# A fused top-k attention and two-layer MLP kernel: the norm's product and low part on GpSimd, another order of VectorE's group, the third transpose in a score bank, layer 2's inputs later

## The chip, the cores and the metric

One Trainium2 chip, one of its cores. A time is the device time of one execution in microseconds (us). The engines are PE (TensorE), DVE (VectorE), ACT (ScalarE), POOL (GpSimd) and SP (SyncE, which here only issues transfers).

## The reference, cut to what matters

```python
def _attn_ref(q, k, v):                       # q, k, v: 4 x 8 x 576 x 64, fp32
    scores = (1 / sqrt(64)) * q @ k.T
    kth = 32nd largest score of each row
    scores = where(scores >= kth, scores, -1e9)
    attn = exp(scores - max(scores))
    attn = attn / (sum(attn) + 1e-9)
    return attn @ v                           # then 2304 tokens x 512
def _moe_ref(x, w_in, w_out, a, b):           # 512 -> 2048 -> 512
    h = x @ w_in
    P = a[0] + a[1]*h + a[2]*h**2 + a[3]*h**3
    Q = 1 + abs(b[0])*abs(h) + abs(b[1])*h**2
    return (P / (Q + 1e-6)) @ w_out
def _moe2_ref(x, w_in, w_out):                # 512 -> 2048 -> 512
    h = x @ w_in
    return (h * cos(h)) @ w_out
```

## The kernel before, in words

Attention runs as 72 **units**: a unit is 128 query rows (tile `t` of two) of a pair of heads (`pr` of four) in one of nine blocks `k` of 256 tokens, so eight units make a block. `qk(i)` forms a unit's scores in `sx`, two PSUM banks that stay in use for the whole kernel: the left half of the 576 keys in bank 0, the right half in bank 1, 288 columns each, first for one head, then for the other; ACT copies them to `sS`. `topk(i)` works on DVE: it writes the elementwise max and min of the two halves into `e`, then alternates MAX8 and MATCH_REPLACE8 four times (the "rank" instructions) until the 32nd value stands, ACT writes exp into `e`, and two SCALAR_TENSOR_TENSOR instructions, the "masks", keep what reaches the 32nd value and sum it. `av(i)` transposes `e` on PE (four 128x128 pieces `pp..a`, four `pp..b` and one, the third, `pp..t`), ACT copies each result to SBUF (`pt..`), and the products with `v` go to free columns of `sx` and from there, through ACT, to `xst` (tile `xs`). After every fourth unit `norm` divides by the row sums: `rs` (DVE), spread to `rx` (ACT), transposed to `bc` on PE in PSUM, `xs` times `bc` (DVE), then a rounded part `xh` (ACT) and the rest `xl`.

The two layers run in groups of 256 hidden columns, one group `g` of each layer per unit, each layer some units behind the attention that feeds it. `mm_in` (lines 480 to 491) is 24 matmuls: `in1` for layer 1, `in2` for layer 2. Layer 1's rational function is `in1`, `pol1`, `mid1` and `end1` (four SCALAR_TENSOR_TENSOR on DVE that end in `u`, "the cubic"; ACT then rounds `u` to `gg`), `low1`, and `out1`, 24 matmuls into `y`. Layer 2's is `in2`, `mid2` (on DVE, behind three ACT steps that end in `n`), a sine on ACT for two groups at a time, `mul2`, `low2`, and `out2`, 12 matmuls into `o`.

**What sets the order.** Every unit has five pieces, p 0 to 4. A table (`timed`, lines 657 to 671) gives each step of the two layers a piece; the attention is a generator that yields once per piece, and a scheduler keeps each engine's order near the order in which code is written. Units 20 to 71 (`U0`, `U1`) are **grouped**: in each, DVE runs its "shared" instructions (max, min, cubic, masks, `mid2`) in one run in the order of the code, then the rank instructions, and every POOL instruction waits for the last shared instruction written before it (classes `InOrder` and `Behind`).

**What waits in queues.** The weights that aren't kept in SBUF come through a ring of four 512 KB buffers (`stream`, tag `st`), filled by SP in the order in which the steps stand in the table: one load each for `in1` (`lo0`), `in2` (`lo1`) and `out1` (`w1ol`), two for `out2` (`w2o`). A load waits until the load four before it has been used. `ps_t` is a ring of two PSUM banks (tag `h`) that `in1`, `in2`, `pp..a`, `pp..b`, `pp..t` and `bc` take in turn; each waits until what stood there two before has been copied out.

Of the kernel before, what the change touches and what calls it, by code (L numbers as in the profile page):

```python
# [10 lines left out]
F32 = mybir.dt.float32  # L11
# [3 lines left out]
AF = mybir.ActivationFunctionType  # L15
# [8 lines left out]
P = 128  # L24
# [4 lines left out]
HALF = S // 2  # L29
# [5 lines left out]
BT = 2 * P  # L35
# [95 lines left out]
def body(tc, out, qt, kt, vt, ident_d, w1_d, w1o_d, a_d, b_d, w2_d, w2o_d):  # L131
# [5 lines left out]
    with ExitStack() as ctx:  # L137
# [186 lines left out]
        def after(mm, bank):  # L324
            for x in order[bank]:
                tc.add_manual_dep(mm.ins, x, mybir.DependencyInfo(mybir.DependencyClass.NoSync, mybir.DependencyReason.DATA), reason="bank")
# [76 lines left out]
        def av(i):  # L403
            n, pr = units[i]
            kvs = ins.pop(i)
            m = P // len(kvs)
            e = et.pop(i).rearrange("p a c -> p (a c)")
            kb, t, bank = n // 2, n % 2, i % 2
            if i % 4 == 0:
                xst[kb, pr // 2] = mo.tile([P, 2, BT], F32, tag="xs", bufs=XB, name=f"xs{kb}_{pr}")  # L410
            xp = sx[:, bank, HALF:HALF + P]

            def tr4(base, nm):
                pp = ps_t.tile([P, 4, P], F32, tag="h", name=f"pp{i}{nm}")
                for c in range(4):
                    PE.transpose(pp[:, c, :], e[:, base + c * P:base + (c + 1) * P], ident)
                pt = att.tile([P, 4, P], F32, tag="pts", bufs=2, name=f"pt{i}{nm}")
                A.activation(pt, pp, AF.Copy)
                return pt

            pj = [tr4(0, "a"), tr4(640, "b")]
            pp = ps_t.tile([P, P], F32, tag="h", name=f"pp{i}t")
            PE.transpose(pp, e[:, 512:640], ident)
            pt = att.tile([P, P], F32, tag="ptt", bufs=1, name=f"pt{i}t")
            A.activation(pt, pp, AF.Copy)
            last = []
            for c, (_, v) in enumerate(kvs):
                qs = slice(c * m, (c + 1) * m)
                mm = PE.matmul(xp[:, qs], v[:, 512:640], pt[:, qs], start=True, stop=False, skip_group_check=True)
                after(mm, bank)  # L430
                for kc in range(4):
                    for j in range(2):
                        o = xp[j * D:(j + 1) * D, qs]
                        mm = PE.matmul(o, v[:, kc * P + j * D:kc * P + (j + 1) * D], pj[j][:, kc, qs], start=False, stop=(kc == 3), skip_group_check=True)  # L434
                        after(mm, bank)
                        if kc == 3:
                            last.append(mm.ins.name)
            order[bank] = last
            A.activation(xst[kb, pr // 2][:, pr % 2, t * P:(t + 1) * P], xp, AF.Copy)

        def norm(kb, hf):
            rs = sml.tile([P, 2, H // 2], F32, tag="rs", bufs=2, name=f"rs{kb}_{hf}")
            V.tensor_scalar_add(rs, sums[kb][:, :, 4 * hf:4 * hf + 4], 1e-9)
            V.reciprocal(rs, rs)
            rx = sml.tile([P, 2, 2, P], F32, tag="rx", bufs=1, name=f"rx{kb}_{hf}")
            A.activation(rx.rearrange("p t c (j d) -> p (t c j) d", j=2), rs.rearrange("p t h -> p (t h)").unsqueeze(2).to_broadcast([P, 8, D]), AF.Copy)
            yield
            bc = ps_t.tile([P, 2, BT], F32, tag="h", name=f"bc{kb}_{hf}")
            for t in range(2):
                for c in range(2):  # L450
                    PE.transpose(bc[:, c, t * P:(t + 1) * P], rx[:, t, c], ident)
            yield
            x = xst.pop((kb, hf))
            V.tensor_mul(x, x, bc)
            yield
            if hf == 0:
                xhl[kb] = [mo.tile([P, NCC, BT], F32R, tag=t, name=f"{t}{kb}") for t in ("xh", "xl")]
            hi, lo = (t[:, 2 * hf:2 * hf + 2] for t in xhl[kb])
            A.activation(hi, x, AF.Copy)
            yield  # L460
            V.tensor_sub(lo, x, hi.bitcast(F32))

        lot, w1t, w2t = {}, {}, {}

# [193 lines left out]
        for k in range(NB):  # L658
            for g in range(NG):
                s1 = S0 + 40 * k + 5 * g  # L660
                s2 = s1 + 5 * LB
                if grouped1(k, g):
                    timed += [(s1, in1, k, g), (s1 + 5, pol1, k, g), (s1 + 9, end1, k, g), (s1 + 10, low1, k, g), (s1 + 11, out1, k, g)]
                else:
                    timed += [(s1, in1, k, g), (s1 + MD, mid1, k, g), (s1 + 5 * L1 - E1P, end1, k, g), (s1 + 5 * L1 + O1P, out1, k, g)]
                if grouped2(k, g):
                    timed += [(s2, in2, k, g), (s2 + 4, mid2, k, g), (s2 + 10, mul2, k, g), (s2 + 12, low2, k, g), (s2 + 13, out2, k, g)]
                else:
                    timed += [(s2 + I2, in2, k, g), (s2 + 5 * L2 + O2, out2, k, g), (s2 + M2P[g % SINB], mul2, k, g)]
            timed.append((s1 + 5 * L1 + SB, sub1, k, 0))  # L670
# [46 lines left out]
        def attention():  # L717
            load_k(1)
            load_v(0)
            qk(0)  # L720
            prev = None
            nrm, fresh, held, low, sq = [], [], [], [], None
            for i in range(nu + 1):
                if LQ == 0 and i % 2 == 0 and i + 2 < nu:
                    load_q(i + 2)
                if i + 1 < nu:
                    qk(i + 1)
                if i + 2 < nu:
                    load_k(i + 2)
                for x, a in held:  # L730
                    store_k(x, *a)
                held = [(prep(*a), a) for a in preps.get(i, [])]
                t = topk(i) if i < nu else iter([None] * 9)
                grouped = U0 <= i < U1
                for p in range(5):
                    if p == 0 and prev is not None and not grouped:
                        next(prev)
                    next(t, None)
                    if p == 0:
                        if grouped:  # L740
                            yield
                            next(prev)
                        if prev is not None:
                            next(prev)
                        if not grouped:
                            next(t, None)
                        for x in low:
                            next(x, None)
                        low = []
                        if prev is not None:  # L750
                            av(i - 1)
                            if i % 4 == 0:
                                nrm.append(norm((i - 1) // 8, (i - 1) // 4 % 2))
                                next(nrm[-1])
                                fresh.append(nrm[-1])
                                if not grouped:
                                    next(nrm[-1])
                        if 0 < i < nu:
                            load_v(i)
                    if p == LQ > 0 and i % 2 == 0 and i + 2 < nu:  # L760
                        load_q(i + 2)
                    if p == SQ and i % 2 == 0 and 8 <= i + 2 < nu:
                        sq = split_q(i + 2)
                        next(sq, None)
                    if p == SQ + 1 and sq is not None:
                        next(sq, None)
                        sq = None
                    if fresh and p == 1 and not grouped:
                        next(fresh.pop())
                    if fresh and grouped and p >= 3:  # L770
                        next(fresh[0])
                        if p == 4:
                            fresh.pop()
                    if len(nrm) == 2 and (p == 1 or p == 4):
                        if not grouped:
                            x = nrm[0 if p == 1 else 1]
                            next(x)
                            next(x, None)
                            if p == 4:
                                nrm = []  # L780
                        elif p == 4:
                            for x in nrm:
                                next(x)
                            low, nrm = nrm, []
                    yield
                prev = t

# [60 lines left out]
```

## Time and profile before

| | |
|---|---|
| median of 3 runs | 1506.75 us (1504.02 to 1507.62) |
| the profiled execution | 1508.62 us, span 1506.8 us |
| PE busy, mean granted clock | 1264.4 us (84%), 0.917 |
| DVE / ACT / POOL busy | 1177.0 / 1092.1 / 549.0 us (78 / 72 / 36%) |
| chain that ended last, by engine | PE 56%, DMA 19%, DVE 15%, ACT 6% |

Matmuls are pipelined, so a busy PE isn't PE at its peak, and PE's clock has two levels, 1.2 and 2.4 GHz: a granted clock of 0.5 is the lower one for the whole stretch. The elementwise work of DVE, ACT and POOL carries line 81, a helper's; its instructions are told apart by their tiles.

### The profile page before, as it was taken

The numbers are of one execution on the slowest core, as the hardware profiler recorded it, in microseconds if no ns is written. First come the engines' busy times: TensorE is split into PE (matmuls) and PEld (weight loads), VectorE is DVE, ScalarE is ACT, GpSimd is POOL, SyncE is SP. The second block draws the span as 40 slices with busy tenths as digits, with TensorE's granted clock in tenths as the row PEclk, the third lists the DMA queues.
The fourth block names the chain that finished last, engine by engine and source line by source line (L and its number), as shares of the span: only waits on it lengthen the run. The fifth ranks groups of instructions, "written<-read, shape, count | busy, mean of one in ns | idle before, by whom it ended". The sixth has DMA issues, their size and how long they took to land.

```text
span 1506.8 us, 24893 instructions
## 1 busy us (share of the span) xinstructions
PE 1264.4 (84%) x8944; PEld 1125.3 (75%) x8944; DVE 1177.0 (78%) x2503; ACT 1092.1 (72%) x1873; POOL 549.0 (36%) x413
## 2 busy tenths in 40 slices
PE   5765776558888988888879888888989898999998
PEld 2443555558777888888878878887878887899986
DVE  6999878998959795979596959786978796947633
ACT  6876877757676777777767778686867776868743
POOL 3566544532434333334333334342433333431000
PEclk9766987778998999999999999999999999999999
DMA  7887768854466655455655564554555776656787
GB/s 245 301 275 228 226 218 269 277 171 139 140 205 200 203 174 200 162 197 173 236 185 194 167 219 168 183 179 172 185 174 199 234 247 232 207 200 226 251 268 234
DMA packets 141548, 314.98 MB, mean 209 GB/s; under 512 B 12016, under 2 KB 28528, under 8 KB 141424
## 3 DMA queue, kind: packets, MB, share of 16 engines
q1 hardware_dynamic: 122832, 261.99, 52.4%
q10 hardware_dynamic: 18592, 51.39, 10.5%
q8 instruction: 71, 1.16, 0.3%
q14 instruction: 53, 0.43, 0.1%
HBM read 278.20 MB, written 35.13 MB: 208 GB/s over the span
## 4 chain that ended last, share of the span: by engine, by line
PE 56%; DMA 19%; DVE 15%; ACT 6%; issue 3%; POOL 1%; ACTq 0%; SPq 0%; DVEq 0%; POOLq 0%
DMA w1ol<-w1ol 11%; PE h L488 9%; PE o L628 9%; PE h L490 8%; PE h L489 8%; DVE e L81 7%; PE y L560 5%; PE y L558 4%; PE sx L434 4%; PE y L559 4%; DVE hd L81 3%; DVE cb L81 2%; DMA raw<-w 2%; DMA out<-ob 2%; DVE u L81 2%
## 5 line engine op out<-in xcount | busy, mean ns | idle before, releaser
L81 DVE MAX8 hd<-e 128x8 f32<-128x288 f32 (+1 forms) x576 | 321.1, 596 | 0.0
L81 DVE MATCH_REPLACE8 e<-hd,e 128x288 f32<-128x288 f32 (+1 forms) x432 | 231.0, 541 | 0.0
L558 PE MATMUL y<-gg,w1o 128*128 128x256 f32 x576 | 177.6, 308 | 54.4 <-ACT gg L81 54.4
L81 POOL TENSOR_TENSOR gg<-u,gg 128x512 fp32r<-128x512 f32 x64 | 83.9, 1311 | 380.3 <-DVE rr L81 93.9
L628 PE MATMUL o<-w2o,gg 128*128 128x512 f32 x864 | 219.4, 394 | 1.6 <-DMA w2o<-w2o 1.5
L560 PE MATMUL y<-gg,w1ol 128*128 128x256 f32 x576 | 175.4, 305 | 51.3 <-DMA w1ol<-w1ol 51.3
L559 PE MATMUL y<-gg,w1o 128*128 128x256 f32 x576 | 174.1, 302 | 6.7 <-POOL gg L81 6.7
L628 PEld LDWEIGHTS o<-w2o,gg 128*128 128x128 f32 x864 | 155.0, 189 | 30.4 <-DMA w2o<-w2o 2.2
L81 DVE TENSOR_TENSOR e<-sS 128x576 f32<-128x576 f32 x144 | 122.7, 891 | 63.8 <-ACT sS L81 58.7
L488 PE MATMUL h<-x2h,w2hi 128*128 128x256 f32 x576 | 167.6, 291 | 2.7 <-ACT pt28b L81 1.3
L488 PE MATMUL h<-xh,w1hi 128*128 128x256 f32 x576 | 169.8, 295 | 0.0
L490 PE MATMUL h<-x2h,lo 128*128 128x256 f32 x576 | 165.1, 287 | 0.3 <-DMA lo<-w2lo 0.3
L490 PE MATMUL h<-xh,lo 128*128 128x256 f32 x576 | 164.9, 286 | 0.0
L489 PE MATMUL h<-xl,w1hi 128*128 128x256 f32 x576 | 164.8, 286 | 0.0
L489 PE MATMUL h<-x2l,w2hi 128*128 128x256 f32 x576 | 164.8, 286 | 0.0
L558 PEld LDWEIGHTS y<-gg,w1o 128*128 128x128 f32 x576 | 118.8, 206 | 59.3 <-ACT gg L81 58.6
L560 PEld LDWEIGHTS y<-gg,w1ol 128*128 128x128 f32 x576 | 118.1, 205 | 59.3 <-DMA w1ol<-w1ol 58.5
L81 POOL TENSOR_TENSOR rr<-rr,hs 128x512 f32<-128x512 f32 x56 | 72.7, 1300 | 166.8 <-DVE rr L81 145.6
L81 POOL TENSOR_TENSOR cb<-cb,raw 128x512 int32<-128x512 int32 x64 | 93.0, 1454 | 99.1 <-DVE cb L81 69.5
L81 DVE SCALAR_TENSOR_TENSOR e<-sS,hd,e 128x576 f32<-128x576 f32 x144 | 125.2, 898 | 4.3 <-ACT e L81 4.2
L559 PEld LDWEIGHTS y<-gg,w1o 128*128 128x128 f32 x576 | 118.0, 205 | 9.5 <-POOL gg L81 9.2
L81 ACT ACTIVATE sS<-sx 128x576 f32<-128x576 f32 x144 | 93.1, 647 | 34.4 <-PE sx L348 15.9
(1167 smaller groups left out, 3641.5 us busy)
## 6 DMA issues: line engine op xcount, KB each, us to landing
w2o<-w2o SPq DMA_DIRECT2D x144, 512.0 KB, 4.4
lo<-w1lo SPq DMA_DIRECT2D x72, 512.0 KB, 4.4
w1ol<-w1ol SPq DMA_DIRECT2D x72, 512.0 KB, 4.6
lo<-w2lo SPq DMA_DIRECT2D x72, 512.0 KB, 4.0
k<-kdr ACTq DMA_DIRECT2D x44, 576.0 KB, 4.8
raw<-w SPq DMA_DIRECT2D x32, 512.0 KB, 5.2
v<-vt ACTq DMA_DIRECT2D x48, 320.0 KB, 4.3
qr<-qt ACTq DMA_DIRECT2D x36, 256.0 KB, 4.2
```

What stands on the lines that cost most here:

```text
L81: r = f(*a, **k)
L434: mm = PE.matmul(o, v[:, kc * P + j * D:kc * P + (j + 1) * D], pj[j][:, kc, qs], start=False, stop=(kc == 3), skip_group_check=True)
L488: PE.matmul(h[:, i, :], wh, xh[:, c, :], start=(c == 0), stop=False)
L489: PE.matmul(h[:, i, :], wh, xl[:, c, :], start=False, stop=False)
L490: PE.matmul(h[:, i, :], lo[:, i, c, :], xh[:, c, :], start=False, stop=(c == NCC - 1))
L558: PE.matmul(y[:, c, :], w1o[:, f, cs], gh[:, i, :], start=(f == 0 and c % 2 == 0), stop=False, skip_group_check=True)
L559: PE.matmul(y[:, c, :], w1o[:, f, cs], gl[:, i, :], start=False, stop=False, skip_group_check=True)
L560: PE.matmul(y[:, c, :], wl[:, i, cs], gh[:, i, :], start=False, stop=(f == NF - 1), skip_group_check=True)
L628: PE.matmul(o[:, t, :], l[:, i, ts], wt[i][:, r], start=(f == 0 and r == 0 and l is gh), stop=(f == NF - 1 and l is gl), skip_group_check= ...
```

## The change

Four edits. **Norm**: in the grouped units ACT copies `bc` from PSUM to an SBUF tile `bs`, and the product and the low part move from DVE to POOL; `bc` is written in p 0 instead of p 3, the product stays in p 4, and the low part comes in p 4 instead of the next unit's p 0. **Group order**: cubic, masks, max, min instead of max, min, cubic, masks. **Third transpose**: it goes to free columns of the score bank that the unit's output does not use, not to the `ps_t` ring. **Layer 2's inputs**: `in2` of grouped units stands two pieces later, so its load falls behind that of `out1`.

```diff
-            pp = ps_t.tile([P, P], F32, tag="h", name=f"pp{i}t")
-            PE.transpose(pp, e[:, 512:640], ident)
+            pp = sx[:, 1 - bank, HALF:HALF + P]
+            mm = PE.transpose(pp, e[:, 512:640], ident)
+            after(mm, 1 - bank)
+            order[1 - bank] = [mm.ins.name]
...
+            pool_norm = U0 <= 8 * kb + 4 * hf + 4 < U1
+            if pool_norm:
+                bs = sml.tile([P, 2, BT], F32, tag="rx", bufs=1, name=f"bs{kb}_{hf}")
+                A.activation(bs, bc, AF.Copy)
             yield
             x = xst.pop((kb, hf))
-            V.tensor_mul(x, x, bc)
+            if pool_norm:
+                G.tensor_mul(x, x, bs)
+            else:
+                V.tensor_mul(x, x, bc)
...
             A.activation(hi, x, AF.Copy)
-            yield
-            V.tensor_sub(lo, x, hi.bitcast(F32))
+            (G if pool_norm else V).tensor_sub(lo, x, hi.bitcast(F32))
...
-                    timed += [(s2, in2, k, g), (s2 + 4, mid2, k, g), (s2 + 10, mul2, k, g), (s2 + 12, low2, k, g), (s2 + 13, out2, k, g)]
+                    timed += [(s2 + I2, in2, k, g), (s2 + 4, mid2, k, g), (s2 + 10, mul2, k, g), (s2 + 12, low2, k, g), (s2 + 13, out2, k, g)]
...
-                    if p == 0 and prev is not None and not grouped:
+                    if p == 0 and grouped:
+                        yield
                         next(prev)
-                    next(t, None)
-                    if p == 0:
-                        if grouped:
-                            yield
-                            next(prev)
+                        next(prev)
+                        next(t)
...
-                    if fresh and grouped and p >= 3:
-                        next(fresh[0])
+                    if len(nrm) == 2 and (p == 4 or p == 1 and not grouped):
+                        for x in nrm if grouped else nrm[:1] if p == 1 else nrm[1:]:
+                            next(x, None)
```

In DVE's order where unit 44 ends and unit 45 begins, `ql46` is the split of a later unit's queries, `xs5_0` the norm's product, `e45` with `sS45` max and min, `u4_2` and `q4_2` the cubic, `e44,sum5` the masks. Before:

```order
L81 TENSOR_TENSOR ql46_8076<-qr46_7964,qh46_8075 128x512
L81 TENSOR_TENSOR xs5_0_7326<-xs5_0_7326,bc5_0_8078 128x512
L81 TENSOR_TENSOR e45_8122<-sS45_7896 128x2x288 x2
L81 SCALAR_TENSOR_TENSOR u4_2_7838<-u4_2_7838,nega_105,w4_2_7835 128x512
L81 SCALAR_TENSOR_TENSOR q4_2_7836<-q4_2_7836,r4_2_7837 128x512
L81 SCALAR_TENSOR_TENSOR u4_2_7838<-u4_2_7838,nega_105,r4_2_7837 128x512
L81 SCALAR_TENSOR_TENSOR u4_2_7838<-q4_2_7836,u4_2_7838 128x512
L81 SCALAR_TENSOR_TENSOR e44_7909,sum5_7092<-sS44_7702,hd_44_7910,e44_7909 128x576 x2
L81 SCALAR_TENSOR_TENSOR rr3_0_7797<-n3_1_8000,rr3_0_7797 128x512
```

and now, at the same place of DVE's queue:

```order
L81 TENSOR_TENSOR ql46_8019<-qr46_7939,qh46_8018 128x512
L81 SCALAR_TENSOR_TENSOR u4_2_7774<-u4_2_7774,nega_105,w4_2_7771 128x512
L81 SCALAR_TENSOR_TENSOR q4_2_7772<-q4_2_7772,r4_2_7773 128x512
L81 SCALAR_TENSOR_TENSOR u4_2_7774<-u4_2_7774,nega_105,r4_2_7773 128x512
L81 SCALAR_TENSOR_TENSOR u4_2_7774<-q4_2_7772,u4_2_7774 128x512
L81 SCALAR_TENSOR_TENSOR e44_7886,sum5_7071<-sS44_7672,hd_44_7887,e44_7886 128x576 x2
L81 TENSOR_TENSOR e45_8100<-sS45_7865 128x2x288 x2
L81 SCALAR_TENSOR_TENSOR rr3_0_7840<-n3_1_8051,rr3_0_7840 128x512
```

The norm's product is gone from the queue, and the cubic follows the rank instructions directly.

In ACT's order around unit 43's transposes and the norm (`rx5_0`, `bs5_0`), the change has these rows, where before `rx5_0` stood a few rows ahead of the copies and there was no `bs`:

```order
L81 ACTIVATE xs5_0_7298<-sx_91 128x128
L81 ACTIVATE rx5_0_7921<-rs5_0_7918 128x512
L81 ACTIVATE pt43a_7896<-pp43a_7891 128x512
L81 ACTIVATE pt43b_7903<-pp43b_7898 128x512
L81 ACTIVATE sS45_7865<-sx_91 128x576
L81 ACTIVATE nb_44_7888<-hd_44_7887 128x2
L81 ACTIVATE bs5_0_7928<-bc5_0_7923 128x512
```

On PE `bc5_0` now stands right behind unit 43's transposes and half of a score product, ahead of `in1`; before it stood inside `out2`, behind `out1`, `in2` and `in1`. So PE needs `rx` early, and the copy that `rx` holds up on ACT is the one that empties the ring for `bc` and `in1`.

On SP, the loads of one unit before (PE uses them in the order `w1ol`, `lo1`, `lo0`, `w2o`, `w2o`):

```order
L467 DMA lo1_3_1_7808<-w2lo_116 128x2x512
L467 DMA lo0_4_3_7847<-w1lo_115 128x2x512
L467 DMA w1ol4_1_7882<-w1ol_118 128x2x512
L467 DMA w2o2_14_7969<-w2o_119 128x1024
L467 DMA w2o2_15_7971<-w2o_119 128x1024
```

and now (PE uses them in the order `lo0`, `w1ol`, `lo1`, `w2o`, `w2o`):

```order
L475 DMA lo0_4_3_7783<-w1lo_115 128x2x512
L475 DMA w1ol4_1_7813<-w1ol_118 128x2x512
L475 DMA lo1_3_1_7851<-w2lo_116 128x2x512
L475 DMA w2o2_14_7949<-w2o_119 128x1024
L475 DMA w2o2_15_7951<-w2o_119 128x1024
```

`lo1` has moved from first to third. `w1ol`, which before took the buffer of the last unit's first `w2o`, now takes that of the last unit's `lo1`.

## Rows read from the trace of the kernel before

**Rows 1.** Busy us (x instructions) of each engine by stretch, PE clock, DMA share, GB/s.

```profile
378.00:1320.00 942.00, 826.86 (x6284) 767.91 (x6283) 752.71 (x1677) 693.36 (x1176) 348.31 (x266) 0.95 0.58 193
1320.00:1507.00 187.00, 178.40 (x1255) 164.69 (x1253) 94.27 (x141) 115.78 (x169) 19.96 (x15) 1.00 0.71 235
```

**Rows 2.** PE's waits from 378 to 1320: us in total, times, longest.

```profile
PE y L558 <- ACT gg L81: 51.0, 13, 5.6
PE y L560 <- DMA w1ol<-w1ol: 50.9, 32, 5.6
```

**Rows 3.** Waits of all engines in the same stretch.

```profile
DVE xs L81 <- PE bc L451: 107.9, 13, 9.7
```

**Rows 4.** DVE in order of time: start, us, what [idle before <-releaser].

```profile
827.59 0.69 DVE L81 TENSOR_TENSOR xs<-xs,bc 128x512 f32<-128x512 f32 x1 [9.53 <-PE bc L451]
828.20 1.42 DVE L81 TENSOR_TENSOR e<-sS 128x576 f32<-128x576 f32 x2
829.54 0.75 DVE L81 SCALAR_TENSOR_TENSOR u<-u,nega,w 128x512 f32<-128x512 f32 x1
832.19 0.81 DVE L81 SCALAR_TENSOR_TENSOR e<-sS,hd,e 128x576 f32<-128x576 f32 x1
```

**Rows 5.** PE in order of time around the same norm.

```profile
826.89 0.60 PE L451 MATMUL bc<-ident,rx 128*128 128x128 f32 x4
...
832.99 0.58 PE L558 MATMUL y<-gg,w1o 128*128 128x256 f32 x1 [3.58 <-ACT gg L81]
```

**Rows 6.** The stretch after that wait; the clock is third from the end.

```profile
832.99:839.60 6.61, 6.27 (x27) 5.85 (x28) 6.61 (x23) 5.13 (x6) 4.84 (x4) 0.50 0.17 64
```

**Rows 7.** PE's waits for `w1ol` in three units running.

```profile
854.12 0.39 PE L560 MATMUL y<-gg,w1ol 128*128 128x256 f32 x1 [0.97 <-DMA w1ol<-w1ol]
...
871.11 0.39 PE L560 MATMUL y<-gg,w1ol 128*128 128x256 f32 x1 [2.40 <-DMA w1ol<-w1ol]
...
887.00 0.38 PE L560 MATMUL y<-gg,w1ol 128*128 128x256 f32 x1 [0.75 <-DMA w1ol<-w1ol]
```

**Rows 8.** Chain that ended last, in order of time: start, us, what.

```profile
800.10 0.12 PE y L558
...
809.03 1.40 PE o L628 x6
810.45 4.97 DMA w1ol<-w1ol
```

**Rows 9.** Tile `w1ol`, 378 to 1320, its transfers.

```profile
DMA to landing us min/median/max: 3.5/4.8/7.4
```

**Rows 10.** ACT's groups, 378 to 1320: busy us, mean ns | idle before.

```profile
L81 ACT ACTIVATE e<-sS,nb 128x576 f32<-128x576 f32 x102 | 75.0, 770 | 1.3 <-DVE hd L81 1.2
...
L81 ACT ACTIVATE n<-rr,magic 128x512 f32<-128x512 f32 x50 | 36.1, 721 | 1.4 <-ACT xs L81 0.2
...
L81 ACT ACTIVATE rx<-rs 128x512 f32<-128x512 f32 x13 | 8.1, 624 | 2.9 <-DVE rs L81 2.1 <-DMA lo<-w2lo 0.7
...
L81 ACT ACTIVATE pt44a<-pp44a 128x512 f32<-128x512 f32 x1 | 0.6, 603 | 0.0
```

**Rows 11.** POOL's and DVE's two-input groups, 378 to 1320 (DVE: by tile, min/median/max ns).

```profile
L81 POOL TENSOR_TENSOR u<-u,w 128x512 f32<-128x512 f32 x52 | 67.3, 1294 | 18.4 <-ACT u L81 18.4
...
L81 DVE TENSOR_TENSOR xs<-xs,bc x13: 687/687/690, 378.0 to 1266.0; 128x512 f32<-128x512 f32 x13
```

**Rows 12.** DVE behind unit 43's masks.

```profile
809.25 0.17 DVE L81 TENSOR_SCALAR rs<-sum 128x8 f32<-128x8 f32 x1
...
809.58 0.64 DVE L81 SCALAR_TENSOR_TENSOR rr<-n,rr 128x512 f32<-128x512 f32 x1
```

**Rows 13.** PE, a unit's transposes to its second half of scores.

```profile
851.45 0.60 PE L416 MATMUL pp45a<-ident,e 128*128 128x128 f32 x4
...
852.45 0.29 PE L346 MATMUL sx<-k,qh 128*128 128x288 f32 x1
```

**Rows 14.** ACT, the third transpose's copy.

```profile
818.15 0.28 ACT L81 ACTIVATE pt43t<-pp43t 128x128 f32<-128x128 f32 x1 [2.00 <-PE pp43t L423]
```

More of the change, by code (lines that the diff above doesn't have):

```diff
@@ L721, in attention @@
             prev = None
-            nrm, fresh, held, low, sq = [], [], [], [], None
+            nrm, fresh, held, sq = [], [], [], None
             for i in range(nu + 1):
@@ L735, in attention @@
                 for p in range(5):
-                    if p == 0 and prev is not None and not grouped:
+                    if p == 0 and grouped:
+                        yield
                         next(prev)
-                    next(t, None)
-                    if p == 0:
-                        if grouped:
-                            yield
-                            next(prev)
+                        next(prev)
+                        next(t)
+                    elif p == 0:
                         if prev is not None:
                             next(prev)
[L745 to L749, printed above, removed]
+                        next(t, None)
+                        if prev is not None:
+                            next(prev)
+                        next(t, None)
+                    else:
+                        next(t, None)
+                    if p == 0:
                         if prev is not None:
@@ L754, in attention @@
                                 next(nrm[-1])
+                                next(nrm[-1])
                                 fresh.append(nrm[-1])
-                                if not grouped:
-                                    next(nrm[-1])
                         if 0 < i < nu:
@@ L767, in attention @@
                         sq = None
-                    if fresh and p == 1 and not grouped:
+                    if fresh and p == (4 if grouped else 1):
                         next(fresh.pop())
-                    if fresh and grouped and p >= 3:
-                        next(fresh[0])
+                    if len(nrm) == 2 and (p == 4 or p == 1 and not grouped):
+                        for x in nrm if grouped else nrm[:1] if p == 1 else nrm[1:]:
+                            next(x, None)
                         if p == 4:
[L773 to L784, printed above, removed]
+                            nrm = []
                     yield
```

## The prediction

> **What bounds the kernel now.** I read the busy time by stretch first. Between 378 and 1320 us, the grouped units, PE is busy 827 of 942 us at a granted clock of 0.95, DVE 753, ACT 693, POOL 348; behind 1320 PE is busy 178 of 187 us at full clock, so little is to be had there [rows 1]. In the grouped stretch the norm's product runs 13 times between 378.0 and 1266.0 us, once in four units [rows 11]: 888 / 48 = 18.5 us per unit, so the 942 us are 50.9 units. Per unit DVE is busy 14.8 us and ACT 13.6. No engine is full, so the next view is PE's waits. Two make nearly all of its 115 idle us: 51.0 us in 13 waits of `out1`'s first product for `gg`, and 50.9 us in 32 waits for the load `w1ol` [rows 2].
>
> The first is the norm. DVE waits 107.9 us in 13 pieces for `bc` [rows 3]. In time: behind unit 44's rank instructions DVE stands 9.53 us before the norm's product at 827.6, because PE reaches `bc` only at 826.9, inside `out2` [rows 4, 5]. Max, min and the cubic queue behind the product; `gg` comes late, and PE stands 3.58 us until 833.0 [rows 5]. Then PE runs at the lower clock: 832.99 to 839.60 was granted 0.50, that is 1.2 GHz, after that idle time [rows 6]. Work of 6.6 us at half clock is 3.3 us lost.
>
> The second is the loads' order. The chain that ended last goes from half of `out2` (809.03 to 810.45) to the `w1ol` transfer (4.97 us) and on to `out1` [rows 8]: the transfer takes the buffer that this half of `out2` frees, `out1` follows within about 3.5 us, and a landing takes 4.8 us in the median, up to 7.4 [rows 9]. That is one to two us in most units. Between them PE can go faster: from 854.12 to 871.11 less its wait of 2.40, and from there to 887.00 less 0.75, are 14.6 and 15.1 us [rows 7]. So a unit without waits costs PE about 14.9 us.
>
> **The change part by part**, summed on the profiled execution's own 1508.6 us, which lies 1.9 above the median of the runs.
>
> *Norm off DVE.* DVE loses 13 products and as many low parts (0.69 us each, 18 us) and the wait for `bc`. The 18 us count nothing, DVE not being full. PE's 51.0 us go, and the slow clock behind them: 3.3 us in the one stretch shown, taken as 3 in each of 13, so 39 (between 0, if the clock falls for another reason, and 43). Term: -90.
>
> *The new wait at `bc`.* `bc` now stands right behind unit 43's transposes and half of a score product. From the first transpose to the end of such a half is about 1.5 us [rows 13]. `rx` needs max and min (829.54 - 828.20 = 1.34), `rs` and its reciprocal (0.33) and its own ACT step (0.62) after the masks' end, and the copy `pt43a`, which empties the ring for `bc`, is queued behind `rx` on ACT (0.60): 2.9 us [rows 4, 10, 12]. Behind it wait `pt43b`, the scores' copy and, on PE, `in1`. So PE stands 1.4 to 2.1 us per norm if it follows the masks at once, 18 to 27 us in all, and nothing if it lags DVE by that much. I take half of the upper end: +13, ends 0 and +27.
>
> *POOL and ACT get work.* 13 products and 13 low parts at 1.29 us are 34 us on POOL, 13 copies `bs` at 0.60 are 8 us on ACT [rows 10, 11]. POOL is idle 594 us of the stretch, ACT 249 [rows 1]; that hides both, and costs 34 us at most if each delayed POOL instruction behind them (`low1`, `mul2`) held up PE. The product waits for the last shared DVE instruction, `mid2`, long past in p 4. I take 0. The Trainium skill (GPSIMD Engine Reference, "4.1 Engine selection") would have such elementwise work on VectorE, since GpSimd is about half as fast with two inputs. The rows agree on the price, 1.29 against 0.69 us [rows 11], by which the move alone would lose 26 x 0.6 = 16 us; by the row of the wait it frees the engine that PE waits for, and my sum goes by the wait.
>
> *Layer 2's inputs later.* The loads now stand in the order in which PE uses them. `w1ol` takes the buffer of `lo1`; from the end of `in2` to the next `out1` lies all of a unit but `in2` and `out1` themselves, 24 products of 0.12 us each [rows 8]: 14.9 - 2 x 2.9 = 9.1 us, over the longest landing of 7.4. So the wait for `w1ol` should go: -51 at best, 0 if another load takes it. I take -43, since SP is one queue and in some units the stores of outputs and keys hold it. The price: `in2` now ends 10.7 us after PE's first transpose (1.5, then `in1`, `out1`, `in2` at 2.9 and half a score product), and `n` follows three ACT steps and one of the cubic's later (0.60 + 0.72 + 0.72 + 0.62 = 2.7: the copy `hs` as `pt44a`, the step for `rr` as that for `n`, the cubic's as `rx` [rows 10]), at 13.4. DVE wants it in `mid2` after its own 14.4 us (14.8 less a quarter of the norm's 1.4) plus max and min, at 15.8. So 2.4 us are spare, and PE's lag behind DVE eats of them. Ends: 0, and one ACT step in each unit, 0.72 x 51 = 37; I take 0.3 per unit, +15.
>
> *Group order.* `gg` and `pp..a` come 1.34 us earlier in DVE's run, exp has 1.34 us less. Rank instructions and masks are still 2.65 us of cubic apart (832.19 - 829.54 [rows 4]), where two exps need 1.5 [rows 10]. I take 0; if the exps came late in each unit it would be 52 x 1.34 = 70 us on DVE, of which its 190 idle us can take most.
>
> *Third transpose.* One fewer user of the ring; in the new order some `out2` products stand between it and the product that needs its copy. The copy is 0.28 us [rows 14] and the transpose as long; hidden, 0; without cover 0.56 x 72 = 40.
>
> Sum: -90 + 13 - 43 + 15 = -105. 1508.6 - 105 = 1403.6, less 1.9: **1402 us**. In the grouped stretch that is 837 / 50.9 = 16.4 us per unit, still 1.5 above PE's 14.9. The stretches before 378 and behind 1320 I leave as they are.
>
> **The rivals.**
>
> *PE becomes the bound, nearly without waits.* For it: the two units without a norm ran at 14.6 and 15.1 [rows 7]. Against it: DVE (14.4) and ACT (13.8 with `bs`) are close behind, and all three are queues in order. At 15.3 us per unit: 50.9 x (18.5 - 15.3) = 163 less, 1344 us on the median's scale. Chance 0.17.
>
> *The load's wait only moves.* `lo0` or the second `w2o`, which takes the buffer that `in1` frees, comes late in place of `w1ol`, and `bc` costs its full price: -90 + 27 + 15 = -48, 1459 us. For it: 193 GB/s now become 193 x 18.5 / 17.5 = 204. Against it: behind 1320 the same queues move 235 GB/s with PE at 95% [rows 1]. Chance 0.17.
>
> *The score bank turns into a handoff per unit (slower).* PE writes the third transpose where ACT reads scores and outputs, so transpose, copy, product, copy and the next scores take turns. If in each unit PE waits for an ACT queue that holds two exps, one copy and the third piece's, that is 1.54 + 0.60 + 0.28 = 2.4 us [rows 10, 14], 174 us in 72 units: -105 + 174 = +69, 1576 us. It decides from 105 / 72 = 1.5 us per unit on. For it: ACT is in order, and exps sit ahead of such copies. Against it: the outputs `xp` share these banks already, and PE's waits on that score are not among its large ones [rows 2]. Chance 0.10. The Trainium skill (PSUM — Partial Sum Buffer, "PSUM bank collisions raise a hardware error") wants semaphores by bank, not by address, by which these turns would be taken whatever the columns. No run here shows yet what they cost.
>
> *No change*, 0.03: DVE's lead is spent on the next wait (scores, `n`) at the same pace.
>
> **How the numbers follow.** Forecast 0.53 at 1402, with 1365 to 1440 as its own range; the rivals 0.17 (1344), 0.17 (1459), 0.10 (1576), 0.03 (1507). About 0.3%, 4.5 us, is what a measurement of this kernel tells from no change. Faster: 0.53 + 0.17 + 0.17 = 0.87; same 0.03; slower 0.10. The range 1350 to 1480 holds the forecast, the moved wait and about two thirds of the case in which PE bounds; it leaves out 0.10 + 0.03 above and 0.05 below.
>
> **What would show it.** In the profile after: no wait of DVE for `bc`, PE's 13 waits for `gg` gone, and the clock of the grouped stretch at 0.98 or more (norm); PE's wait for `w1ol` under 10 us with no other load in its place (loads); PE waiting for `rx` or for a `pt..a` copy at `bc`, 13 times, under 27 us in all; DVE's waits for `n` under 40 us; PE's waits for ACT at the third transpose and at `av` under 20 us. The prediction is wrong if PE's idle time in the grouped stretch stays near 100 us under other names, or if a wait on the score banks appears in every unit.

## The result, and the profile after

The changed kernel runs in 1385.88 us (median of 4 runs, 1385.39 to 1386.85), against 1507.18 us before (also 4 runs): a ratio of 0.919, 95% interval 0.915 to 0.922. The forecast was 1402, its range 1350 to 1480. The profiled execution took 1386.08 us, its span is 1384.3.

The busy times by stretch answer to [rows 1]. The grouped units now lie between 363 and 1195 us; columns as there.

```profile
363.00:1195.00 832.00, 799.78 (x6375) 744.48 (x6377) 759.65 (x1670) 693.22 (x1205) 389.61 (x296) 0.99 0.66 221
1195.00:1384.00 189.00, 178.79 (x1265) 165.35 (x1261) 94.25 (x147) 118.00 (x173) 18.27 (x14) 1.00 0.71 235
```

PE is idle for 32 us of the stretch instead of 115, and its clock is granted at 0.99 instead of 0.95. The stretch behind it is as it was. The pace can be read from one instruction, the `rs` of each norm: before, the first and the last of the 13 in the grouped units ran at 365.02 and 1244.39 us, now at 362.95 and 1133.29. For 48 units that is 18.32 and 16.05 us per unit, so 109 of the 122 us lie here; 2 lie before the first, 6 in the four units behind the last, 6 in what follows. Over these 48 units PE's idle time falls from 107.4 to 31.6 us and its busy time from 772.0 to 738.8, with the clock granted at 0.99 instead of 0.95; the rows stand in the part on the prediction.

PE's waits in the grouped stretch answer to [rows 2]:

```profile
PE y L567 <- POOL gg L81: 7.0, 6, 2.7
PE o L636 <- POOL gg L81: 4.2, 10, 0.8
...
PE bc L453 <- ACT rx L81: 1.3, 2, 1.1
...
PE y L568 <- DMA w1ol<-w1ol: 1.0, 1, 1.0
```

The 51.0 us for `gg` from ACT and the 50.9 us for `w1ol` are gone, and the largest wait left is 7.0 us for the low part that POOL makes. DVE's waits answer to [rows 3]; none is for `bc`:

```profile
DVE ql L81 <- ACT qh L81: 40.5, 13, 8.7
DVE e L81 <- PE sx L423: 12.6, 6, 3.3
DVE q L81 <- ACT r L81: 10.2, 13, 1.0
DVE e L81 <- ACT e L81: 4.5, 8, 1.0
DVE rr L81 <- ACT n L81: 2.2, 3, 1.2
```

On POOL the norm's product waits for something else than it did on DVE: not for `bc` but for ACT's last copy of the outputs into `xs`. PE's largest wait for anything that POOL makes is the 7.0 us above. The product's own wait, columns as in [rows 2]:

```profile
POOL xs L81 <- ACT xs L81: 34.2, 7, 6.0
```

DVE and PE in order of time around the norm of unit 44 answer to [rows 4, 5, 12]. DVE first:

```profile
747.21 1.42 DVE L81 TENSOR_TENSOR e<-sS 128x576 f32<-128x576 f32 x2
748.55 0.16 DVE L81 TENSOR_SCALAR rs<-sum 128x8 f32<-128x8 f32 x1
...
756.68 0.67 DVE L81 TENSOR_TENSOR ql<-qr,qh 128x512 fp32r<-128x512 f32 x1
757.27 0.74 DVE L81 SCALAR_TENSOR_TENSOR u<-u,nega,w 128x512 f32<-128x512 f32 x1
```

and PE:

```profile
748.65 0.66 PE L416 MATMUL pp43a<-ident,e 128*128 128x128 f32 x4
749.27 0.60 PE L416 MATMUL pp43b<-ident,e 128*128 128x128 f32 x4
749.62 0.38 PE L346 MATMUL sx<-k,qh 128*128 128x288 f32 x1
...
750.25 0.60 PE L453 MATMUL bc<-ident,rx 128*128 128x128 f32 x4
```

Where DVE stood 9.53 us it goes from the query split into the cubic at once. PE starts on unit 43's transposes 1.4 us after DVE's masks are done (max and min begin at 747.21), so `rx`, made from `rs`, is ready when PE comes to `bc` at 750.25.

### The profile page after: what moved, and what is told of

The parts are those of the page before. It is cut to its first block, busy times and chain, and to the rows that moved or that the text cites. A ratio compares the mean times of both kernels' runs of the same rounds, so it can differ in the third digit from the quotient of the medians.

```text
span 1384.3 us, 24846 instructions
## 1 busy us (share of the span) xinstructions
PE 1233.5 (89%) x8944; PEld 1095.6 (79%) x8944; DVE 1170.6 (85%) x2477; ACT 1080.4 (78%) x1886; POOL 589.7 (43%) x439
## 4 chain that ended last, share of the span: by engine, by line
PE 41%; DVE 25%; ACT 15%; DMA 9%; issue 5%; POOL 5%; ACTq 0%; SPq 0%; POOLq 0%; DVEq 0%
DVE e L81 11%; PE o L636 8%; DVE hd L81 5%; PE h L496 5%; PE h L498 5%; PE h L497 5%; DVE u L81 4%; PE y L567 3%; PE sx L436 3%; PE y L568 3%; PE y L566 2%; DMA raw<-w 2%; POOL gg L81 2%; ACT r L81 2%; ACT L81 2%
## 5 line engine op out<-in xcount | busy, mean ns | idle before, releaser
L567 PE MATMUL y<-gg,w1o 128*128 128x256 f32 x576 | 167.4, 291 | 9.2 <-POOL gg L81 9.1
L566 PE MATMUL y<-gg,w1o 128*128 128x256 f32 x576 | 170.7, 296 | 2.9 <-ACT gg L81 2.9
L568 PE MATMUL y<-gg,w1ol 128*128 128x256 f32 x576 | 166.3, 289 | 2.1 <-DMA w1ol<-w1ol 2.1
L496 PE MATMUL h<-x2h,w2hi 128*128 128x256 f32 x576 | 162.9, 283 | 0.0
L81 DVE TENSOR_TENSOR e<-sS 128x576 f32<-128x576 f32 x144 | 116.5, 849 | 29.1 <-PE sx L423 21.7
L496 PEld LDWEIGHTS h<-xh,w1hi 128*128 128x128 f32 x576 | 114.8, 199 | 24.8 <-ACT pt10a L81 3.2
L81 POOL TENSOR_TENSOR cb<-cb,raw 128x512 int32<-128x512 int32 x64 | 93.0, 1456 | 75.2 <-DVE cb L81 68.0
L567 PEld LDWEIGHTS y<-gg,w1o 128*128 128x128 f32 x576 | 113.5, 197 | 11.4 <-POOL gg L81 10.9
L566 PEld LDWEIGHTS y<-gg,w1o 128*128 128x128 f32 x576 | 113.3, 197 | 4.5 <-ACT gg L81 3.4
L568 PEld LDWEIGHTS y<-gg,w1ol 128*128 128x128 f32 x576 | 113.4, 197 | 3.3 <-DMA w1ol<-w1ol 2.5
```

What stands on the lines that cost most here:

```text
L81: r = f(*a, **k)
L496: PE.matmul(h[:, i, :], wh, xh[:, c, :], start=(c == 0), stop=False)
L566: PE.matmul(y[:, c, :], w1o[:, f, cs], gh[:, i, :], start=(f == 0 and c % 2 == 0), stop=False, skip_group_check=True)
L567: PE.matmul(y[:, c, :], w1o[:, f, cs], gl[:, i, :], start=False, stop=False, skip_group_check=True)
L568: PE.matmul(y[:, c, :], wl[:, i, cs], gh[:, i, :], start=False, stop=(f == NF - 1), skip_group_check=True)
```

## The experiments

The first four undo one edit each in the changed kernel; the next four make one edit alone in the kernel before, or only the order of the loads; the last four come from what these showed. A ratio is to the kernel before on the same chip, with its 95% interval; on the chips used here the median of the kernel before is 1507 to 1512 us.

**The norm undone (`u_norm`).** The norm as it was, the other three edits kept:

```diff
-                G.tensor_mul(x, x, bs)
+            V.tensor_mul(x, x, bc)
...
-            (G if pool_norm else V).tensor_sub(lo, x, hi.bitcast(F32))
+            yield
+            V.tensor_sub(lo, x, hi.bitcast(F32))
...
+                    if fresh and grouped and p >= 3:
+                        next(fresh[0])
```

> The changed kernel (1386 us) with the norm as before: product and low part on VectorE, bc in p 3; the other three edits stay. My theory, two separate waits: VectorE waits for bc again, 8 to 10 us in 13 norms, PE waits for gg behind it and runs on at the lower clock; 70 to 90 us back, 1456 to 1476 us. Rival, the ring and the group order carry the gain: with the third transpose out of the ring, bc comes earlier and the wait stays small; under 25 us back, below 1411 us.

Measured: 1399.37 us (0.9275, 0.9244 to 0.9305), 13 us above the changed kernel: my range of 1456 to 1476 fell, and the rival's mark, below 1411, is met. PE waits 24.8 us for `gg`, DVE 48.4 us in 9 waits, now for `xs`:

```profile
PE y L560 <- ACT gg L81: 24.8, 8, 4.4
```

```profile
DVE xs L81 <- ACT xs L81: 48.4, 9, 7.5
```

The norm's term of -90 is not what the norm's edit brings here. The row names `ACT xs` where [rows 3] named `bc`. PE's order, read from the two programs, has the reason: `bc` stands 24 matmuls of the layers behind unit 43's transposes (24 to 48 in all norms counted), not 71 to 83 as before, though the norm's code is the old one. The other three edits had already moved it.

**Layer 2's inputs undone (`u_in2`).**

```diff
-(s2 + I2, in2, k, g), (s2 + 4, mid2, k, g)
+(s2, in2, k, g), (s2 + 4, mid2, k, g)
```

> The changed kernel with layer 2's inputs at their old piece; the other three edits stay. My theory: the loads stand again as lo1, lo0, w1ol, PE waits for w1ol in most units, 40 to 50 us in all; 35 to 50 us back, 1421 to 1436 us. Rival, the waits for w1ol came from PE's order around the norm's stalls and not from the order of the loads: under 15 us back, and PE's wait for w1ol under 15 us.

Measured: 1393.03 us (0.9232, 0.9202 to 0.9263), 7 us back, against 35 to 50 expected; the rival's marks, under 15 us of time and of wait, are met. PE's wait for `w1ol`:

```profile
PE y L568 <- DMA w1ol<-w1ol: 11.3, 10, 2.5
```

The loads stand in the old order, and still `w1ol` is mostly in time: in PE's order 17 to 65 products (single matmuls) of `in1` and `in2` now stand between `out2` and the first use of `w1ol` in 35 of 44 units counted, where before 35 of 44 had none.

**The third transpose undone (`u_tr`).**

```diff
-            pp = sx[:, 1 - bank, HALF:HALF + P]
-            mm = PE.transpose(pp, e[:, 512:640], ident)
+            pp = ps_t.tile([P, P], F32, tag="h", name=f"pp{i}t")
+            PE.transpose(pp, e[:, 512:640], ident)
```

> The changed kernel with the third transpose in the ring of two banks again; the other three edits stay. My theory: the transpose's place was worth nothing, 1381 to 1395 us. Rival, the ring carries part of the gain: bc, in1 and in2 wait for one more copy in each unit, 0.5 us or more per unit, 26 us or more back, 1412 us or above.

Measured: 1400.41 us (0.9269, 0.9236 to 0.9302), 15 us back, between my theory's range and the rival's. DVE's largest wait is then for `n`, the one that I had priced for `in2`:

```profile
DVE rr L81 <- ACT n L81: 75.3, 36, 6.0
```

**The group order undone (`u_order`).**

```diff
                     if p == 0 and grouped:
+                        next(t)
                         yield
                         next(prev)
                         next(prev)
-                        next(t)
```

> The changed kernel with VectorE's group in its old order, max, min, cubic, masks; the other three edits stay. My theory: worth nothing, 1381 to 1395 us, as VectorE has idle time. Rival: the cubic 1.34 us later in each of 52 units holds up gg and out1 each time, up to 70 us back; 1410 us or above if a third of that reaches PE.

Measured: 1384.66 us (0.9172, 0.9144 to 0.9201): nothing, as expected.

So the four undoings give back 13, 7, 15 and -1 us of 121, by medians on two chips. By the ratios it is 13, 6, 12 and -3, and only the first and the third stand clear of the changed kernel's interval. Either the parts cure the same losses, or the losses are one. The next four ask which.

**The norm alone (`o_norm`).** The edit on `norm` and its places in the attention loop, in the kernel before.

> The kernel before with the norm's edit alone. PE's order then has out1 directly behind out2 still (in most units no product of in1 or in2 lies between them), bc 17 to 29 products behind the transposes instead of 71 to 83. Theory A, two separate losses, each with its cure: the norm's loss goes (80 to 100 us), the wait for w1ol stays at 40 us or more; 1410 to 1435 us. Theory B, after the four single undoings (-1 to +14 us): the losses are coupled, each edit also loosens PE's order, and any one takes most of the gain; below 1405 us.

Measured: 1457.32 us (0.9632, 0.958 to 0.9684), -54 us. PE's three largest waits:

```profile
PE y L566 <- DMA w1ol<-w1ol: 65.5, 37, 4.1
PE sx L346 <- ACT sS L81: 9.1, 9, 2.6
PE y L564 <- ACT gg L81: 1.7, 2, 1.2
```

`gg` is cured, but `w1ol` has grown from 50.9 us in 942 to 65.5 in the 832 us of this window. Theory B falls; theory A has the mechanism, and its size of 80 to 100 us was too large. DVE's wait for ACT's copy of the scores, `sS`, grows too, from 44.5 us in 13 waits to 75.0 in 21.

**Layer 2's inputs later, alone (`o_in2`).** The line of `u_in2`, made in the kernel before.

> The kernel before with layer 2's inputs later, alone. In PE's order 24 products then lie between out2 and the first use of w1ol, bc stands 47 products behind the transposes instead of 71 to 83, and the product is on VectorE. Theory A: the wait for w1ol goes (-40 to -50) and the norm's loss stays in most part; 1440 to 1470 us. Theory B, coupled: below 1420 us.

Measured: 1382.38 us (0.9143, 0.9105 to 0.918), -129 us: the whole change, from one edit. That is below theory B's mark of 1420, and theory A's 1440 to 1470 fell. PE's waits and then DVE's:

```profile
PE y L558 <- ACT gg L81: 3.6, 4, 2.2
PE y L559 <- POOL gg L81: 2.5, 6, 0.5
PE y L560 <- DMA w1ol<-w1ol: 1.1, 2, 0.7
```

```profile
DVE rr L81 <- ACT n L81: 35.5, 26, 2.8
DVE xs L81 <- PE bc L451: 16.6, 10, 2.9
```

Both of PE's waits are gone, and DVE's for `bc` falls from 107.9 to 16.6 us with the product still on DVE. The timeline of one norm, DVE and then PE:

```profile
748.12 0.17 DVE L81 TENSOR_SCALAR rs<-sum 128x8 f32<-128x8 f32 x1
...
758.27 0.69 DVE L81 TENSOR_TENSOR xs<-xs,bc 128x512 f32<-128x512 f32 x1 [1.33 <-PE bc L451]
```

```profile
747.55 0.60 PE L416 MATMUL pp43a<-ident,e 128*128 128x128 f32 x4
...
757.56 0.60 PE L451 MATMUL bc<-ident,rx 128*128 128x128 f32 x4
```

DVE comes to the product 8.8 us after `rs` (758.27 - 1.33 - 748.12), the rank instructions later. `bc` comes 10.0 us after the first transpose, behind `in1` and `out1`, 47 products. In the kernel before `in2` and part of `out2` stood ahead of it as well; the first transpose was at

```profile
812.25 0.60 PE L416 MATMUL pp43a<-ident,e 128*128 128x128 f32 x4
```

and `bc` at 826.89 [rows 5], 14.6 us. With `in2` behind `bc`, `bc` is nearly in time. So one edit reaches both losses, which by itself doesn't say whether they are one or two.

**The loads alone (`o_loads`).** No step moved, only `out1`'s load ahead of `in2`'s and `in1`'s:

```diff
+        for j in range(len(loads) - 2):
+            if loads[j + 2][1] is load_w1ol and loads[j][1] is load_lo and loads[j + 1][1] is load_lo and grouped1(*loads[j + 2][2:]):
+                loads[j:j + 3] = [loads[j + 2], loads[j], loads[j + 1]]
```

> The kernel before, only the order of the loads changed: out1's load first, then in2's and in1's, as PE uses them; the steps keep their pieces, and PE's order stays (out1 directly behind out2, bc 71 to 77 products behind the transposes). Theory A: the wait for w1ol goes by itself, -40 to -50 us; 1457 to 1467 us. Rival: what w1ol no longer waits for, another load does, or the norm's wait grows by as much; 1490 us or above.

Measured: 1447.63 us (0.9583, 0.9547 to 0.9619), -64 us, more than theory A's 40 to 50. This lies outside both expected ranges, on the good side. PE has no wait for `w1ol` left in this stretch, and the norm's loss stays:

```profile
PE y L558 <- ACT gg L81: 40.7, 12, 5.0
```

```profile
DVE xs L81 <- PE bc L451: 88.0, 12, 8.1
```

That the order of the loads makes the wait for `w1ol` is shown by this run on its own: nothing else was edited, and `out1` still stands directly behind `out2` in 35 of 44 units.

**The third transpose alone (`o_tr`).** The diff of `u_tr` reversed, in the kernel before.

> The kernel before with the third transpose in the score bank, alone. PE's order then has 24 or 48 products of in1 and in2 between out2 and the first use of w1ol in most units (before: none), bc still 71 products behind the transposes. My prediction's term for this edit is 0: 1500 to 1510 us. Theory A': it cures the wait for w1ol through PE's order and leaves the norm's loss; 1450 to 1470 us. Theory B, coupled: below 1420 us.

Measured: 1456.41 us (0.9632, 0.9598 to 0.9666), -55 us, where my term was 0 and theory A' said 1450 to 1470:

```profile
PE y L560 <- ACT gg L81: 39.9, 17, 5.0
PE y L562 <- DMA w1ol<-w1ol: 11.2, 9, 3.5
```

It cures most of the wait for `w1ol` with the loads in their old order, and only PE's order has changed around them: 24 or 48 products stand ahead of the first use in 36 of 44 units. Most of the norm's loss stays: DVE waits 59.2 us for `bc`.

**Both cures, no step moved (`l_norm`).** The edits of `o_loads` and `o_norm` together.

> The kernel before with two edits: the loads in PE's order (as in the run on the loads alone, -64 us) and the norm's edit (alone -54 us). Steps keep their pieces, out1 stays directly behind out2 in every unit. If the two losses are separate they add up: 1512 - 64 - 54 = 1394 us, 1385 to 1405. If they are one loss seen from two sides, the second cure brings little: 1435 us or above.

Measured: 1400.14 us (0.9287, 0.926 to 0.9314), -109 against -118 for the sum of the two. The losses are two, and they nearly add.

**The same with the product on VectorE (`l_dve`).** `bc` as early, copied to `bs` as in `l_norm`, but:

```diff
-                G.tensor_mul(x, x, bs)
+                V.tensor_mul(x, x, bs)
...
-            (G if pool_norm else V).tensor_sub(lo, x, hi.bitcast(F32))
+            V.tensor_sub(lo, x, hi.bitcast(F32))
```

> As the kernel with both cures, but the norm's product and low part on VectorE; bc is copied to SBUF as early (23 to 25 products behind the transposes). Theory: the place of bc counts, not the engine. VectorE gets 1.37 us per norm back and no wait for bc: within 10 us of the kernel with both cures. Rival: the product has to leave VectorE, whose run of shared instructions sets the pace, 20 us or more above it.

Measured: 1426.43 us (0.9454, 0.9427 to 0.9481), 26 us above `l_norm`. My "within 10 us" fell, and the rival's size is right. Its reason is not what the rows show. DVE is hardly fuller (707 us busy over 48 units, 702 in `l_norm`), but stands in line:

```profile
DVE xl L81 <- ACT xh L81: 35.1, 6, 6.1
DVE xs L81 <- ACT xs L81: 28.6, 12, 4.2
```

```profile
PE y L564 <- ACT gg L81: 33.8, 7, 6.5
```

With the low part directly behind ACT's rounding, DVE waits 35.1 us for `xh`, six times, each ahead of the two low parts of a block, and 28.6 us for `xs`, with the cubic queued behind, and PE's wait for `gg` is back. That is partly my edit's doing: the kernel before left the low part for the next unit. On POOL the same product waits too (40.6 us for `xs` in `l_norm`) and PE doesn't notice. So in this pair the engine does count, by whose queue the norm's waits stand in. The faster engine (0.69 against 1.29 us for one such instruction, [rows 11]) makes the slower kernel by 26 us, because it is the one waited for. The Trainium skill (GPSIMD Engine Reference, "4.1 Engine selection") would have this work on VectorE for its speed; the rows agree on the speed, and the pair goes the other way. It isn't so in every order: in `o_in2` the product is on DVE too, waits 16.6 us for `bc`, and the kernel is at 1382.

**One edit beside four, on one chip (`r_in2`, `r_after`).**

> The kernel before with layer 2's inputs later, alone, again, now beside the changed kernel on one chip. Theory: this edit cures both losses (loads in PE's order, and bc 47 instead of 71 to 83 products behind the transposes, before VectorE comes to the product), and the other three edits add nothing to it: 0 to 6 us below the changed kernel. Rival: the 4 us between them lay in the chips; within 1 us or above.

> The changed kernel again, as the neighbour of the kernel with one edit: 1383 to 1390 us.

Measured: 1381.43 us (0.916, 0.9133 to 0.9186) with layer 2's inputs later alone, 1383.81 (0.9185, 0.9157 to 0.9214) with all four edits. The intervals overlap: the two are the same, as far as this shows, and the kernel with one edit is 2.4 us ahead in the medians, as it was 3.5 us ahead on the chips before. No kernel run here is clearly faster than the changed one.

## Why the prediction was right, and which of its steps were not

The sum was right: -105 forecast, -121 measured, with the two losses named beforehand and both gone from the rows that had shown them. How it was shared out among the edits was wrong. PE's time over the 48 units from the first to the last `rs` (columns as in [rows 1], nearly the same number of matmuls in each) tells idle from busy; in this order, the kernel before, `o_loads`, `o_norm`, `l_norm`, the changed kernel and `o_in2`:

```profile
365.02:1244.39 879.37, 772.02 (x5810) 716.30 (x5810) 702.90 (x1572) 650.58 (x1105) 322.36 (x246) 0.95 0.57 191
367.11:1184.14 817.03, 758.63 (x5814) 707.01 (x5814) 703.70 (x1572) 646.75 (x1105) 320.95 (x246) 0.96 0.62 206
365.58:1200.34 834.76, 752.38 (x5800) 700.09 (x5800) 705.28 (x1549) 647.19 (x1115) 354.88 (x270) 0.97 0.61 201
365.31:1141.63 776.32, 743.31 (x5812) 689.07 (x5812) 701.68 (x1548) 646.53 (x1117) 353.91 (x270) 0.99 0.65 217
362.95:1133.29 770.34, 738.75 (x5815) 686.35 (x5817) 704.11 (x1550) 643.86 (x1119) 355.46 (x270) 0.99 0.65 219
365.17:1128.17 763.00, 746.04 (x5830) 686.09 (x5829) 709.63 (x1572) 639.87 (x1108) 328.44 (x246) 1.00 0.67 221
```

Of the 109 us that these units lose, 76 are idle time and 33 busy time. The prediction's sum has 94 us of waits gone, 39 for the clock and 28 for new waits, which is 66 and 39. So for the four edits together the mechanism holds in kind and size, and the nearness isn't mere luck; which edit cures which loss is where the terms fail.

- *Norm off DVE, -90.* The mechanism holds, the size does not. Alone it brings 54 us: over the 48 units PE's idle time falls by 25 us, because PE, freed of one wait, runs into the other (`w1ol` 65.5 us), and its busy time by 20, at a clock of 0.97 instead of 0.95, where the term had 39 for the clock. As one of four edits it brings 13, since the other three, `in2`'s new place among them, cure most of it too. The step that failed is "PE's 51.0 us go, and the slow clock behind them", taken in full for an edit that stands beside others.
- *Layer 2's inputs later, -43 + 15.* The order of the loads brings 64 us alone. I took the 51 us of waits as the best that could come of it; over the 48 units idle time falls by 49 us and busy time by 13, at a clock of 0.96 instead of 0.95; the term had nothing for the clock. The step missed altogether that moving `in2` also brings `bc` forward: alone it is worth 129 us. The price of 15 us for `n` did not come: DVE waits 2.2 us for it in the changed kernel and 35.5 in `o_in2`, where PE, busy 746.0 of 763.0 us, doesn't feel it.
- *The new wait at `bc`, +13 (0 to 27).* 1.3 us in two waits, the lower end: around unit 44 PE follows the masks 1.4 us late, and `rx` has that time.
- *POOL and ACT get work, 0.* POOL went from 348 to 390 us busy. PE's waits for POOL's `gg` are 11 us in all.
- *Group order, 0.* -1 us when undone, within the noise.
- *Third transpose, 0.* Alone 55 us, undone 15. I priced its copy and its bank and not what its leaving the ring does to PE's order. The program with this edit alone would have shown that beforehand; I read the order of the four together only.
- *The rivals.* The load's wait did not move to another load. The score bank's handoff did not come: DVE waits 12.6 us for the third transpose, and PE's waits at that transpose for ACT's reading of the scores are 11.3 us in the whole execution, all of them before the grouped units. PE all but bound (1344) is the nearest: the pace is 16.05 us, not 15.3 and not 16.4. But its floor of 14.9 us per unit, read from the two units of [rows 7], is too low: in `o_in2`, at a clock of 1.00, PE's busy time alone is 746.0 / 48 = 15.5 us per unit, and the pace 15.9.

The order of the programs is what joins these. For each kernel: how many of 44 grouped units have no product of `in1` or `in2`, or at most six, between `out2` and the first use of `w1ol`; how many matmuls of the layers stand between a unit's transposes `pp..b` and `bc` (norms of units 24 to 68); the order of the loads; and the time:

```
          none between   ahead of bc   order of the loads    median us
before         35          71 to 83    in2, in1, out1        1507
o_loads        35          71 to 77    out1, in2, in1        1448
o_tr            8          71 to 72    in2, in1, out1        1456
o_norm         37          17 to 29    in2, in1, out1        1457
l_dve          42          18 to 25    out1, in2, in1        1426
l_norm         44          23 to 25    out1, in2, in1        1400
u_tr           24           0 to 1     in1, out1, in2        1400
u_norm         11          24 to 48    in1, out1, in2        1399
u_in2           9           0 to 1     in2, in1, out1        1393
after           7           0 to 1     in1, out1, in2        1386
u_order        12           0          in1, out1, in2        1385
o_in2          13          47 to 50    in1, out1, in2        1382
```

In these kernels a load is in time if its place among the loads fits PE's order, by moving either; the norm's wait for `bc` goes, or nearly so, with 50 matmuls or fewer ahead of `bc`, and stays with 71 or more. Every kernel with one of the two cured is near 1450, every kernel with both at 1400 or below, but for `l_dve`, in which DVE waits for something else. What makes the last 18 us between 1400 and 1382 was not separated. In `l_norm`, against `o_in2`, it shows as PE's idle time (33.0 and 17.0 us over the 48 units), and PE's largest wait there is for ACT's copy of the scores:

```profile
PE sx L346 <- ACT sS L81: 17.5, 16, 2.5
```

## What to carry to other kernels

When several edits are made at once, read the order of each program with one edit alone before pricing them apart: here one line in a table of due times moved a load, a transpose and a wait of another engine, and was worth as much as all four edits. A queue's loads should stand in the order in which they are used. A step that waits belongs in a queue with nothing urgent behind it, or after what it waits for.

## What the runs showed of the hardware that was not expected

The clock didn't go by the sum of PE's idle time. Over the 48 units `o_norm` has 82 us of it and was granted 0.97, `o_loads` has 58 us and was granted 0.96. In the kernel before, the six microseconds behind two of the waits for `w1ol` in [rows 7], 0.97 and 2.40 us long, were granted full clock (third from the end), where the 3.58 us for `gg` had left 0.50 [rows 6]:

```profile
854.12:860.00 5.88, 5.88 (x51) 5.76 (x53) 5.78 (x9) 2.85 (x6) 0.95 (x1) 1.00 0.50 164
871.11:877.00 5.89, 5.89 (x48) 5.89 (x49) 1.47 (x3) 4.75 (x11) 2.12 (x2) 1.00 0.28 97
```

Over the grouped units of that kernel the five microseconds behind 12 of PE's 13 waits for `gg` (2.2 to 5.6 us) were granted 0.50 to 0.71, and 1.00 behind the other one; behind the waits for `w1ol` of 1.0 to 1.8 us it was 1.00 each time, and behind longer ones either. So here a few long waits took more of the clock than many short ones.
